# Keeping three more quarter tiles of the KV cache between two layers, two of them in PSUM

## The chip, the cores and the metric

The kernel runs on one core of a Trainium2 chip. A core has a matmul engine (TensorE, PE; its weight loads are listed as PEld), a vector engine (VectorE, DVE), a scalar engine (ScalarE, ACT), a general engine (GpSimd, POOL) and a queue engine that here issues all the DMAs (SyncE, SP). SBUF is the working memory of 128 partitions; PSUM is the memory that matmuls write to, 128 partitions of eight banks of 2 KB. The metric is the device time of one execution in microseconds, lower is better.

## The reference

Two equal layers of a decoder step for a batch of 8, one new token each, width 640, 32 heads of 128, a cache of 4096 positions and one key/value head per query head. Both layers use the same cache and the same weights:

```python
x = x + attention(layernorm(x), k_cache, v_cache, wq, wo)   # q = x @ wq; softmax(q k / sqrt(128)) v; @ wo
x = x + relu(layernorm(x) @ w1) @ w2                         # 640 -> 1728 -> 640
x = x + attention(layernorm(x), k_cache, v_cache, wq, wo)
x = x + relu(layernorm(x) @ w1) @ w2
```

K and V are 268 MB each in bf16. Everything else is small: the weights are 15 MB together. A batch entry's layer 1 needs that entry's layer 0 finished, but different entries do not depend on each other.

## The kernel before

**Tiles.** Heads are taken in 16 pairs (`hp`). K or V of one pair of one batch entry is a tile of 128 partitions x 8192 bf16, 2 MB, cut in four *granules* of 512 KB (4 KB in each partition). On the host the cache is laid out so that the tiles of one entry lie in the order in which they are read. In SBUF lies one `arena` of 26 granule slots; `A_kv` is loaded into it by `do_load(b, p, n, u)`, n granules in a row from place p of entry b into slots u onward. A granule of K costs PE 16 weight loads and 16 matmuls of one column (L490), a granule of V four matmuls of 512 columns in four column groups (L478).

**Visits.** One head pair of one entry in one layer is a visit; there are 256. Layer 0 takes the pairs 0 to 15, layer 1 takes them as 15, 14, 13, 0, 1, ... 12. After layer 0 of entry b come the first four visits of layer 0 of entry b+1, then layer 1 of entry b, then the rest of layer 0 of b+1. The last two entries are cut a little differently, so that layer 0 of the last entry is followed by four visits of the entry before it.

**Around a visit.** The scores of a K tile go to `s_ps` (two buffers). `M1` takes the maxima per partition (DVE), `T` transposes them on PE, `M2` reduces them (DVE), `B` spreads them (PE), `E` makes the exponentials (ACT), `L` and `I` the sums and their reciprocals (PE, DVE). While this chain runs, PE reads the V tile of the visit before. After a V tile `OC` copies the sums out of `o_ps` (ACT), `OG` and `O` gather and scale them, `W` and `Y` apply `wo` and add to x. At the end of an entry's layer 0 the two layernorms and the feed-forward run as *finishing steps*, in pieces of some 15 matmuls between granules, with the inverse root on POOL; then `Q` and `QC` make the queries of layer 1, two visits ahead.

**The order is written by a planner.** `plan()` runs on the host and emits one list of operations. `stream` is the order in which granules are wanted: K of a visit, then V of the visit before. `feed()` walks along it: it takes as many granules as `LEADS` allows for the time by which the modelled load clock is ahead of the modelled PE clock (8 with 9 us of lead, 4 with 6, 2 with 5, else 1), as far as they are neighbours in memory and alike in being kept or not, looks for that many free slots in a row (`room`), and emits one load. If there is no room it stops until the next `release`. `release` is called after each granule's matmuls; it frees the slot unless the granule is kept. All engines execute in the order of this list, so SP's queue is in that order too: a load whose slot is still being read holds up the loads behind it. The DMAs signal through eight semaphores in turn, and a load also waits for the load eight places ahead of it.

**What is kept.** `keep` names granules that stay in their slots from the entry's layer 0 to its layer 1 and are not read a second time. They are `G - SPARE` = 21: V and K of pair 15, V and K of pair 14, V of pair 13 and one granule of K of pair 13. While they lie there, between the end of an entry's layer 0 and the first visits of its layer 1, five slots are left for the first four visits of the next entry.

**PSUM.** Seven of eight banks are used: `o_ps`, two of `s_ps`, and one each of `blk_ps`, `q_ps`, `oy_ps` and `ch_ps`, whose tiles are made anew for each use.

```python
            most = next((n for least, n in LEADS if clock[1] - clock[0] >= least), 1)
            most = min(most, max(1, (len(stream) - at[0]) // 2))
            b, p, keeping = place(stream[at[0]])
```

Of the kernel before, what the change touches and what calls it, by code (L numbers as in the profile page):

```python
# [9 lines left out]
FP32 = mybir.dt.float32  # L10
# [6 lines left out]
UNIT = 4  # L17
GP = 4
G = 26
SPARE = 5  # L20
LEADS = ((9, 8), (6, 4), (5, 2))
AHEAD = 4
CAP = 20


def tile_at(NP, which, hp):

    return max(0, 2 * hp - 1) if which == "K" else min(2 * hp + 2, 2 * NP - 1)


def plan(B, NP, n_up, n_down):
# [18 lines left out]
    assert NV == 2 * B * NP and NP % GP == 0  # L50
    last_of = {(layer, b): v for v, (layer, b, hp) in enumerate(visits)}

    keep = set()
    for hp in order1:
        for which in "VK":
            for g in range(UNIT - 1, -1, -1):
                if len(keep) < G - SPARE:
                    keep.add((which, hp, g))

    slots = []  # L60
    for i in range(NV + 1):
# [22 lines left out]
    def keeps(which, i, g):  # L84
        return visits[i][0] == 0 and (which, visits[i][2], g) in keep

    def place(x):

        return visits[x[1]][1], tile_at(NP, x[0], visits[x[1]][2]) * UNIT + x[2], keeps(*x)

    def room(n):
# [4 lines left out]
    def feed():  # L96

        while at[0] < len(stream):
            most = next((n for least, n in LEADS if clock[1] - clock[0] >= least), 1)
            most = min(most, max(1, (len(stream) - at[0]) // 2))  # L100
            b, p, keeping = place(stream[at[0]])
            n = 1
            while n < most and place(stream[at[0] + n]) == (b, p + n, keeping):
                n += 1
            u = room(n)
            if u is None:
                return
            for k, (which, i, g) in enumerate(stream[at[0] : at[0] + n]):
                ops.extend(("weights",) + w for w in weights.pop(i, []) if which == "K")
                owner[u + k] = True  # L110
                where[which, i, g] = u + k
                if keeping:
                    kept[which, b, visits[i][2], g] = u + k
            clock[1] = max(clock[1], clock[0] + 1.4) + 0.1 + 1.2 * n
            lands[u : u + n] = [clock[1] + 2] * n
            ops.append(("load", b, p, n, u))
            at[0] += n

    def find(which, i, g):
        u = where.get((which, i, g))  # L120
# [2 lines left out]
    def release(which, i, g):  # L123
        key = which, visits[i][1], visits[i][2], g
        u = where.pop((which, i, g), None)
        if key in kept:
            if visits[i][0] == 0:
                return
            u = kept.pop(key)
        at[1] += 1  # L130
        owner[u], freed[u] = False, at[1]
        feed()
# [91 lines left out]
def kernel(  # L224
# [91 lines left out]
    arena = kv.tile([P, G * GW], BF16, name="arena")  # L316
    OR = 96 + CJ
    o_ps = ps.tile([P, CJ * Dh], FP32, name="o_ps")
    nc.vector.memset(o_ps, 0.0)

    up_parts = [range(f, min(f + 3, FC)) for f in range(0, FC, 3)]
# [3 lines left out]
    def ln_steps(b0, nb, xln, key):  # L325
        x = xT[:, b0 : b0 + nb, :]

        def sums():
            s1 = st[key, "s1"] = sm.tile([P, nb], FP32, name="s1", bufs=1)
            nc.vector.tensor_reduce(out=s1, in_=x, axis=AX.X, op=ALU.add)  # L330

        def mean():
            st[key, "mean"] = ps.tile([P, nb], FP32, name="ch_ps")
            nc.tensor.matmul(st[key, "mean"], lhsT=ones_f, rhs=st[key, "s1"], start=True, stop=True)

        def center():
            xc = st[key, "xc"] = sm.tile([P, nb, DC], FP32, name="xc", bufs=1)
            nc.vector.scalar_tensor_tensor(
                out=xc, in0=_free(st[key, "mean"], [(1, nb), (0, DC)]), scalar=-1.0 / D, in1=x, op0=ALU.mult, op1=ALU.add
            )  # L340
            sq = sm.tile([P, nb, DC], FP32, name="sq", bufs=1)
            nc.vector.tensor_tensor(out=sq, in0=xc, in1=xc, op=ALU.mult)
            s2 = st[key, "s2"] = sm.tile([P, nb], FP32, name="s2", bufs=1)
            nc.vector.tensor_reduce(out=s2, in_=sq, axis=AX.X, op=ALU.add)

        def var():
            st[key, "var"] = ps.tile([P, nb], FP32, name="ch_ps")
            nc.tensor.matmul(st[key, "var"], lhsT=ones_f, rhs=st[key, "s2"], start=True, stop=True)  # L348

        def scale():  # L350
            rstd = sm.tile([P, nb], FP32, name="rstd", bufs=1)
            if nb == 1:
                inverse_root(rstd, st[key, "var"])
                nc.gpsimd.tensor_scalar(  # L354
                    out=xln[:, 0, :], in0=st[key, "xc"][:, 0, :], scalar1=rstd, scalar2=None, op0=ALU.mult
                )
            else:
                std = sm.tile([P, nb], FP32, name="std", bufs=1)
                nc.scalar.activation(out=std, in_=st[key, "var"], func=ACT.Sqrt, bias=eps_c, scale=1.0 / D)
# [23 lines left out]
    def finish_steps(layer, b):  # L383
# [5 lines left out]

        def up(k):  # L390
            if k == 0:
                st[key, "h"] = ps.tile([P, FC, nb], FP32, name="ch_ps")
            for f in up_parts[k]:
                fs = f_sizes[f]
                for c in range(DC):
                    nc.tensor.matmul(  # L396
                        st[key, "h"][:fs, f, :], lhsT=w1_sb[:, c, f * P : f * P + fs], rhs=xf[:, :, c],
                        start=(c == 0), stop=(c == DC - 1),
                    )
# [8 lines left out]

        def down(c):
            if c == 0:  # L410
                st[key, "y"] = ps.tile([P, DC, nb], FP32, name="ch_ps")
            for f, fs in enumerate(f_sizes):
                nc.tensor.matmul(
                    st[key, "y"][:, c, :], lhsT=w2_sb[:fs, f, c * P : (c + 1) * P],
                    rhs=st[key, "hT"][:fs, f, :], start=(f == 0), stop=(f == FC - 1),
                )
# [16 lines left out]
    def do_finish(layer, b, k, op):  # L433
# [5 lines left out]
        else:  # L439
            steps[steps[2]][op]()  # L440
            steps[2] = steps[2] or op == "add"

    def do_load(b, p, n, u):
        nc.sync.dma_start(out=arena[:, u * GW : (u + n) * GW], in_=A_kv[b, :, p * GW : (p + n) * GW])

    def do_q0(g):

        q_ps = ps.tile([P, 2 * GP, B], FP32, name="q_ps")
        for h in range(2 * GP):
            for c in range(DC):  # L450
                nc.tensor.matmul(
                    q_ps[:, h, :], lhsT=wq_sb[:, g, c, h * Dh : (h + 1) * Dh], rhs=xln0[:, :, c],
                    start=(c == 0), stop=(c == DC - 1),
                )
        nc.scalar.copy(out=q0[:, g * 2 * GP : (g + 1) * 2 * GP, :], in_=q_ps)

    def do_q(b, hp):
        q_ps = st["q", b, hp] = ps.tile([P, 2], FP32, name="q_ps")
        g, n = divmod(hp, GP)
        for h in range(2):  # L460
            for c in range(DC):
                nc.tensor.matmul(  # L462
                    q_ps[:, h : h + 1], lhsT=wq_sb[:, g, c, (2 * n + h) * Dh : (2 * n + h + 1) * Dh],
                    rhs=xlns[b][:, 0, c : c + 1], start=(c == 0), stop=(c == DC - 1),
                )
# [6 lines left out]
    def do_mm(which, i, g, u):  # L472
# [9 lines left out]
                )  # L482
            return
        if g == 0:
            s_tiles[i] = ps.tile([P, 2 * NJ], FP32, name="s_ps", bufs=2)
        h = 2 * hp + g * 2 // UNIT
        q = q1[b][:, h : h + 1] if layer else q0[:, h, b : b + 1]
        for n in range(GJ):
# [7 lines left out]
        nc.vector.tensor_reduce(out=m_tiles[i], in_=s_tiles[i].rearrange("p (h j) -> p h j", h=2), axis=AX.X, op=ALU.max)  # L496

    def do_t(i):
        blk[i] = ps.tile([P, P + 2 + 2 * NJ], FP32, name="blk_ps")
        nc.tensor.matmul(blk[i][:2, :P], lhsT=m_tiles.pop(i), rhs=ident, start=True, stop=True)  # L500

    def do_m2(i):
# [33 lines left out]
        nc.scalar.copy(out=o_tiles[i][:OR], in_=o_ps[:OR, :].rearrange("p (j d) -> p j d", j=CJ))  # L536

    def do_og(i):
        oy[i] = ps.tile([P, 2 + DC * B], FP32, name="oy_ps")
        for j in range(CJ):  # L540
            nc.tensor.matmul(  # L541
                oy[i][:, :2], lhsT=o_tiles[i][:OR, j, :], rhs=gsel[:OR, j, :], start=(j == 0), stop=(j == CJ - 1)
            )
# [19 lines left out]
    def do_y(i):  # L563
# [2 lines left out]
        y = oy.pop(i)[:, 2 : 2 + DC * nb].rearrange("p (c b) -> p b c", b=nb)  # L566
        nc.vector.tensor_tensor(out=xT[:, b0 : b0 + nb, :], in0=xT[:, b0 : b0 + nb, :], in1=y, op=ALU.add)

    does = dict(load=do_load, weights=load_weights, mm=do_mm, M1=do_m1, T=do_t, M2=do_m2, B=do_b, E=do_e,
                L=do_l, I=do_i, OC=do_oc, OG=do_og, O=do_o, W=do_w, Y=do_y, C=do_finish, Q0=do_q0, Q=do_q, QC=take_q)  # L570

    with tc.manual_schedule(engines={ENG.PE, ENG.DVE, ENG.Activation, ENG.Pool, ENG.SP}):
        xT_ps = ps.tile([P, B * DC], FP32, name="ch_ps")
        nc.tensor.matmul(xT_ps, lhsT=x_bf, rhs=ident[: B * DC, : B * DC], start=True, stop=True)
        nc.vector.tensor_copy(out=xT, in_=xT_ps.rearrange("p (b c) -> p b c", b=B))
        xln0 = consts.tile([P, B, DC], BF16, name="xln0")
# [1 line left out]
            step()  # L578
        for op in ops:
            does[op[0]](*op[1:])  # L580
        r_ps = ps.tile([B * DC, P], FP32, name="ch_ps")
        nc.tensor.matmul(r_ps, lhsT=outT.rearrange("p b c -> p (b c)"), rhs=ident, start=True, stop=True)
        xo = sm.tile([B * DC, P], BF16, name="xo", tag="row", bufs=1)
        nc.vector.tensor_copy(out=xo, in_=r_ps)
# [53 lines left out]
```

## Time and profile before

| | |
|---|---|
| time, median of 3 runs | 2401.72 us (2396.83 to 2401.98) |
| the profiled execution | 2403.26 us, span 2401.5 us |
| TensorE clock granted | 1.0 |
| PE, PEld, DVE, ACT, POOL busy | 1279.5, 786.7, 350.9, 341.2, 43.2 us |
| read from HBM | 1000.66 MB, 417 GB/s over the span |
| loads of the arena | 597, of 1 to 8 granules; 312 of one, 125 of eight |
| issue to landing, median | 6.4 us (one granule), 23.5 (four), 25.0 (eight) |

The page lists busy time by engine, then the span in 40 slices of 60 us with a digit for the busy share in tenths, and for DMA the rate in GB/s. A line of instruction groups reads: line of the program, engine, operation, output and input tiles, count, then busy time and mean, and the idle time before them with what ended it. The chain of work that ended last is followed backwards from the last instruction: at each step to what released it, or to the instruction before it on its engine. A line of the chain in order of time has a start, a duration and what ran; `DMA arena<-in_A_kv_dram` is the time from the issue of a load to its landing. A line of a table of stretches has the stretch, its length, the busy time of each engine with the number of instructions, the granted clock, the busy share of the DMA engines and GB/s.

### The profile page before, as it was taken

How to read it: one execution, taken by the hardware profiler on the slowest of the kernel's cores; microseconds unless marked ns; L12 is line 12 of the kernel's file. 1: busy time of each engine (PE TensorE's matmuls, PEld its weight loads, DVE VectorE, ACT ScalarE, POOL GpSimd, SP SyncE). 2: the span in 40 equal slices, each digit the busy share in tenths (PEclk: the TensorE clock that was granted, in tenths of full speed). 3: DMA queues.
4: the chain of work that ended last, by engine and by line, in shares of the span. 5: the costliest groups of instructions: out<-in, count | busy, mean ns of one | idle time of the engine just before them, and what ended most of it. 6: DMA issues, size and time to landing. Idle time of an engine off the chain costs nothing.

```text
span 2401.5 us, 57352 instructions
## 1 busy us (share of the span) xinstructions
PE 1279.5 (53%) x26486; PEld 786.7 (33%) x26486; DVE 350.9 (15%) x1792; ACT 341.2 (14%) x1179; POOL 43.2 (2%) x198
## 2 busy tenths in 40 slices
PE   3436644475444754447444574445744457445845
PEld 2224322243322532225222352223422234222523
DVE  1101111121111211112111121111111111111211
ACT  1111111111111111111111111111111111111111
POOL 0000000000000000000000000000000000000000
DMA  9999999999999999999999999999999999999997
GB/s 411 431 429 394 429 430 432 428 393 433 430 433 427 371 432 429 432 418 394 434 428 431 416 398 434 430 433 406 413 431 432 430 400 415 431 433 414 406 433 307
DMA packets 87749, 1004.38 MB, mean 418 GB/s; under 512 B 9812, under 2 KB 9812, under 8 KB 49748
## 3 DMA queue, kind: packets, MB, share of 16 engines
q1 hardware_dynamic: 87508, 1000.71, 98.8%
q8 instruction: 207, 3.39, 0.5%
q14 instruction: 34, 0.28, 0.0%
HBM read 1000.66 MB, written 0.01 MB: 417 GB/s over the span
## 4 chain that ended last, share of the span: by engine, by line
DMA 81%; PE 14%; DVE 1%; ACT 1%; issue 1%; POOL 1%; SPq 0%; ACTq 0%; DVEq 0%; POOLq 0%
DMA arena<-in_A_kv_dram 81%; PE o_ps L478 6%; PE s_ps L490 5%; ACT o_sb L536 1%; DVE hmx L504 1%; PE q_ps L462 1%; PE oy_ps L541 1%; PE blk_ps L509 0%; DVE diag L506 0%; PE oy_ps L558 0%; PE blk_ps L500 0%; POOL root L378 0%; DMA wq_sb<-in_A_wq_dram 0%; PE ch_ps L396 0%; PE ch_ps L348 0%
## 5 line engine op out<-in xcount | busy, mean ns | idle before, releaser
L478 PE MATMUL o_ps<-arena,P_sb 128*4 128x512 bf16 x4096 | 562.0, 603 | 506.9 <-DMA arena<-in_A_kv_dram 504.5
L490 PEld LDWEIGHTS <-arena 128*128 128x128 bf16 x16384 | 497.6, 105 | 575.2 <-DMA arena<-in_A_kv_dram 569.0
L490 PE MATMUL s_ps<-q_96,arena 128*128 128x1 bf16 x8192 | 274.0, 165 | 350.1 <-DMA arena<-in_A_kv_dram 346.8
L478 PEld LDWEIGHTS <-P_sb 128*4 128x4 bf16 x4096 | 99.3, 83 | 584.1 <-issue 577.1
L513 ACT ACTIVATE nmax<-blk_ps 128x2 f32<-128x2 f32 x256 | 44.1, 172 | 1702.7 <-PE blk_ps L509 1702.7
L536 ACT CAST o_sb<-o_ps 100x512 bf16<-100x512 f32 x256 | 150.0, 586 | 193.7 <-PE o_ps L478 193.7
L528 DVE TENSOR_REDUCE lsum<-blk_ps 128x2 f32<-128x64 f32 x256 | 57.6, 225 | 731.2 <-PE blk_ps L522 731.2
L496 DVE TENSOR_REDUCE mrow<-s_ps 128x2 bf16<-128x64 f32 x256 | 57.7, 225 | 471.7 <-PE s_ps L490 471.6
L517 ACT ACTIVATE P_sb<-s_ps,nmax 128x32 bf16<-128x32 f32 x512 | 119.3, 284 | 8.2
L504 DVE TENSOR_REDUCE hmx<-blk_ps 2x1 f32<-2x128 f32 x256 | 71.4, 279 | 266.1 <-PE blk_ps L500 265.2
L522 PEld LDWEIGHTS <-onesb_c 128*128 128x128 bf16 x256 | 26.6, 104 | 199.5 <-issue 199.5
L500 PE MATMUL blk_ps<-ident,mrow 128*2 128x128 bf16 x256 | 78.6, 307 | 0.2 <-PE o_ps L478 0.2
L541 PE MATMUL oy_ps<-gsel,o_sb 100*128 100x2 bf16 x1024 | 66.1, 168 | 18.3 <-ACT o_sb L536 0.7
L509 PEld LDWEIGHTS <-onesb_c 2*128 2x128 bf16 x256 | 25.1, 98 | 129.6 <-issue 129.6
L551 DVE TENSOR_TENSOR oT<-oy_ps,invL 128x2 bf16<-128x2 f32 x128 | 20.4, 160 | 321.6 <-PE oy_ps L541 321.6
L522 PE MATMUL blk_ps<-P_sb,onesb_c 128*128 128x64 bf16 x256 | 60.0, 234 | 1.1 <-ACT P_sb L517 1.1
L490 PE MATMUL s_ps<-q_19385,arena 128*128 128x1 bf16 x1024 | 32.8, 166 | 50.7 <-DMA arena<-in_A_kv_dram 50.5
L541 PEld LDWEIGHTS <-o_sb 100*128 100x128 bf16 x1024 | 47.4, 106 | 31.5 <-ACT o_sb L536 31.0
L490 PE MATMUL s_ps<-q_23500,arena 128*128 128x1 bf16 x1024 | 34.0, 166 | 42.1 <-DMA arena<-in_A_kv_dram 41.8
L490 PE MATMUL s_ps<-q_11143,arena 128*128 128x1 bf16 x1024 | 32.6, 166 | 41.5 <-DMA arena<-in_A_kv_dram 41.2
L509 PE MATMUL blk_ps<-diag,onesb_c 2*128 2x2 bf16 x256 | 42.1, 164 | 22.5 <-DVE diag L506 0.2
L462 PE MATMUL q_ps<-xq,wq_sb 128*128 128x1 bf16 x1280 | 52.1, 165 | 3.1 <-POOL xq L354 2.7
(176 smaller groups left out, 703.8 us busy)
## 6 DMA issues: line engine op xcount, KB each, us to landing
arena<-in_A_kv_dram SPq DMA_DIRECT2D x125, 4096.0 KB, 25.0
arena<-in_A_kv_dram SPq DMA_DIRECT2D x104, 2048.0 KB, 23.5
arena<-in_A_kv_dram SPq DMA_DIRECT2D x312, 512.0 KB, 6.4
arena<-in_A_kv_dram SPq DMA_DIRECT2D x41, 1024.0 KB, 11.9
arena<-in_A_kv_dram SPq DMA_DIRECT2D x5, 3584.0 KB, 24.1
arena<-in_A_kv_dram SPq DMA_DIRECT2D x8, 1536.0 KB, 22.4
wq_sb<-in_A_wq_dram SPq DMA_DIRECT2D x4, 1280.0 KB, 29.9
wo_sb<-in_A_wo_dram SPq DMA_DIRECT2D x4, 1280.0 KB, 29.9
```

The costliest lines, as they stand in the source:

```text
L462: nc.tensor.matmul(q_ps[:, h : h + 1], lhsT=wq_sb[:, g, c, (2 * n + h) * Dh : (2 * n + h + 1) * Dh], rhs=xlns[b][:, 0, c : c + 1], start=( ...
L478: nc.tensor.matmul(o_ps[32 * c : 32 * c + CJ, :], lhsT=P_tiles[i][:, h, j : j + CJ], rhs=arena[:, at + c * CJ * Dh : at + (c + 1) * CJ * D ...
L490: nc.tensor.matmul(s_tiles[i][:, j : j + 1], lhsT=arena[:, at + n * P : at + (n + 1) * P], rhs=q, start=True, stop=True)
L496: nc.vector.tensor_reduce(out=m_tiles[i], in_=s_tiles[i].rearrange("p (h j) -> p h j", h=2), axis=AX.X, op=ALU.max)
L500: nc.tensor.matmul(blk[i][:2, :P], lhsT=m_tiles.pop(i), rhs=ident, start=True, stop=True)
L504: nc.vector.tensor_reduce(out=hmx, in_=blk[i][:2, :P], axis=AX.X, op=ALU.max)
L509: nc.tensor.matmul(blk[i][:, P : P + 2], lhsT=ones_b, rhs=nmax.pop(i), start=True, stop=True)
L517: nc.scalar.activation(out=P_tiles[i][:, h, :], in_=S[:, h, :], func=ACT.Exp, bias=nm[:, h : h + 1], scale=inv_sqrt_dh)
L522: nc.tensor.matmul(blk[i][:, P + 2 :], lhsT=ones_p, rhs=P_tiles[i].rearrange("p h j -> p (h j)"), start=True, stop=True)
L528: nc.vector.tensor_reduce(out=L, in_=blk.pop(i)[:, P + 2 :].rearrange("p (h j) -> p h j", h=2), axis=AX.X, op=ALU.add)
L536: nc.scalar.copy(out=o_tiles[i][:OR], in_=o_ps[:OR, :].rearrange("p (j d) -> p j d", j=CJ))
L541: nc.tensor.matmul(oy[i][:, :2], lhsT=o_tiles[i][:OR, j, :], rhs=gsel[:OR, j, :], start=(j == 0), stop=(j == CJ - 1))
```

## The change

- `SPARE` is 4, so 22 granules are kept in the arena, and `STASH` = 2 more granules of each entry are kept in PSUM. The order of what is kept is now K15, K14, V15, K13, V14, V13, from the first granule of each: 22 in SBUF are K15, K14, V15, K13, V14 and two granules of V13; the other two of V13 go to PSUM. No granule of these three pairs is read again for layer 1.
- After the matmuls of a stashed granule in layer 0, `do_stash` copies it to two PSUM tiles (DVE, as int32 with an OR of zero, two instructions of 128x512), and only then is the slot free. When the stream of layer 1 comes to it, `feed` emits `unstash` in place of a load: into a free slot, half by ACT and half by DVE (128x1024 bf16 each).
- The small PSUM tiles are made once and cut from three banks: both halves of `s_ps` in one, `blk_ps` with the queries in the second, `oy_ps` with the layernorm, feed-forward, first and last transposes in the third. With `o_ps` that is four banks; the other four hold the stash.
- The length of a load is also bounded by room: at most a third of the slots that are not kept, less two (8 with nothing kept, 1 with 20 or more).

By the built program there are 625 loads of the arena (333 of one granule, 57 of two, 10 of three, 99 of four, 12 of six, 1 of seven, 113 of eight) against 597, and 1856 granules loaded against 1880. The instructions on PE are the same in number; DVE has 48 more, ACT 16 more (two instructions for each of 16 stashed granules going in, one on each engine coming out).

```diff
@@ -17,9 +17,11 @@
 UNIT = 4
 GP = 4
 G = 26
-SPARE = 5
+SPARE = 4
+STASH = 2
 LEADS = ((9, 8), (6, 4), (5, 2))
 AHEAD = 4
+BANK = 512
 CAP = 20
 
 
@@ -50,12 +52,12 @@
     assert NV == 2 * B * NP and NP % GP == 0
     last_of = {(layer, b): v for v, (layer, b, hp) in enumerate(visits)}
 
-    keep = set()
-    for hp in order1:
-        for which in "VK":
-            for g in range(UNIT - 1, -1, -1):
-                if len(keep) < G - SPARE:
-                    keep.add((which, hp, g))
+    first = [("K", order1[0])]
+    for n in range(3):
+        first += [("K", order1[n + 1])] * (n < 2) + [("V", order1[n])]
+    first = [(which, hp, g) for which, hp in first for g in range(UNIT)]
+    keep = set(first[: G - SPARE])
+    stash = first[G - SPARE : G - SPARE + STASH]
 
     slots = []
     for i in range(NV + 1):
@@ -84,8 +86,15 @@
     def keeps(which, i, g):
         return visits[i][0] == 0 and (which, visits[i][2], g) in keep
 
+    def stashed(which, i, g):
+
+        x = which, visits[i][2], g
+        return stash.index(x) if x in stash else None
+
     def place(x):
 
+        if visits[x[1]][0] and stashed(*x) is not None:
+            return None, stashed(*x), False
         return visits[x[1]][1], tile_at(NP, x[0], visits[x[1]][2]) * UNIT + x[2], keeps(*x)
 
     def room(n):
@@ -97,10 +106,10 @@
 
         while at[0] < len(stream):
             most = next((n for least, n in LEADS if clock[1] - clock[0] >= least), 1)
-            most = min(most, max(1, (len(stream) - at[0]) // 2))
+            most = min(most, max(1, (len(stream) - at[0]) // 2), max(1, (G - len(kept) - 2) // 3))
             b, p, keeping = place(stream[at[0]])
             n = 1
-            while n < most and place(stream[at[0] + n]) == (b, p + n, keeping):
+            while n < most and b is not None and place(stream[at[0] + n]) == (b, p + n, keeping):
                 n += 1
             u = room(n)
             if u is None:
@@ -111,10 +120,14 @@
                 where[which, i, g] = u + k
                 if keeping:
                     kept[which, b, visits[i][2], g] = u + k
+            at[0] += n
+            if b is None:
+                lands[u] = clock[0] + 2
+                ops.append(("unstash", p, u))
+                continue
             clock[1] = max(clock[1], clock[0] + 1.4) + 0.1 + 1.2 * n
             lands[u : u + n] = [clock[1] + 2] * n
             ops.append(("load", b, p, n, u))
-            at[0] += n
 
     def find(which, i, g):
         u = where.get((which, i, g))
@@ -127,6 +140,8 @@
             if visits[i][0] == 0:
                 return
             u = kept.pop(key)
+        if visits[i][0] == 0 and stashed(which, i, g) is not None:
+            ops.append(("stash", stashed(which, i, g), u))
         at[1] += 1
         owner[u], freed[u] = False, at[1]
         feed()
@@ -316,6 +331,11 @@
     arena = kv.tile([P, G * GW], BF16, name="arena")
     OR = 96 + CJ
     o_ps = ps.tile([P, CJ * Dh], FP32, name="o_ps")
+    s_ps = ps.tile([P, 2, 2 * NJ], FP32, name="s_ps")
+    blk_ps = ps.tile([P, BANK], FP32, name="blk_ps")
+    oy_ps = ps.tile([P, BANK], FP32, name="oy_ps")
+    stash_ps = [ps.tile([P, 2 * BANK], BF16, name=f"stash{n}_ps") for n in range(STASH * GW // (2 * BANK))]
+    per = len(stash_ps) // STASH
     nc.vector.memset(o_ps, 0.0)
 
     up_parts = [range(f, min(f + 3, FC)) for f in range(0, FC, 3)]
...
@@ -440,12 +460,25 @@
             steps[steps[2]][op]()
             steps[2] = steps[2] or op == "add"
 
+    def do_stash(slot, u):
+        for n, t in enumerate(stash_ps[slot * per : (slot + 1) * per]):
+            nc.vector.tensor_scalar(
+                out=t.bitcast(mybir.dt.int32),
+                in0=arena[:, u * GW + n * 2 * BANK : u * GW + (n + 1) * 2 * BANK].bitcast(mybir.dt.int32),
+                scalar1=0, scalar2=None, op0=ALU.bitwise_or,
+            )
+
+    def do_unstash(slot, u):
+        for n, t in enumerate(stash_ps[slot * per : (slot + 1) * per]):
+            copy = nc.vector.tensor_copy if n % 2 else nc.scalar.copy
+            copy(out=arena[:, u * GW + n * 2 * BANK : u * GW + (n + 1) * 2 * BANK], in_=t)
+
     def do_load(b, p, n, u):
         nc.sync.dma_start(out=arena[:, u * GW : (u + n) * GW], in_=A_kv[b, :, p * GW : (p + n) * GW])
 
     def do_q0(g):
 
-        q_ps = ps.tile([P, 2 * GP, B], FP32, name="q_ps")
+        q_ps = blk_ps[:, 256 : 256 + 2 * GP * B].rearrange("p (h b) -> p h b", b=B)
         for h in range(2 * GP):
             for c in range(DC):
                 nc.tensor.matmul(
@@ -455,7 +488,7 @@
         nc.scalar.copy(out=q0[:, g * 2 * GP : (g + 1) * 2 * GP, :], in_=q_ps)
 
     def do_q(b, hp):
-        q_ps = st["q", b, hp] = ps.tile([P, 2], FP32, name="q_ps")
+        q_ps = st["q", b, hp] = blk_ps[:, 320:322]
         g, n = divmod(hp, GP)
         for h in range(2):
             for c in range(DC):
@@ -482,7 +515,7 @@
                 )
             return
         if g == 0:
-            s_tiles[i] = ps.tile([P, 2 * NJ], FP32, name="s_ps", bufs=2)
+            s_tiles[i] = s_ps[:, i % 2]
         h = 2 * hp + g * 2 // UNIT
         q = q1[b][:, h : h + 1] if layer else q0[:, h, b : b + 1]
         for n in range(GJ):
@@ -496,7 +529,7 @@
         nc.vector.tensor_reduce(out=m_tiles[i], in_=s_tiles[i].rearrange("p (h j) -> p h j", h=2), axis=AX.X, op=ALU.max)
 
     def do_t(i):
-        blk[i] = ps.tile([P, P + 2 + 2 * NJ], FP32, name="blk_ps")
+        blk[i] = blk_ps[:, : P + 2 + 2 * NJ]
         nc.tensor.matmul(blk[i][:2, :P], lhsT=m_tiles.pop(i), rhs=ident, start=True, stop=True)
 
     def do_m2(i):
@@ -536,7 +569,7 @@
         nc.scalar.copy(out=o_tiles[i][:OR], in_=o_ps[:OR, :].rearrange("p (j d) -> p j d", j=CJ))
 
     def do_og(i):
-        oy[i] = ps.tile([P, 2 + DC * B], FP32, name="oy_ps")
+        oy[i] = oy_ps[:, : 2 + DC * B]
         for j in range(CJ):
             nc.tensor.matmul(
                 oy[i][:, :2], lhsT=o_tiles[i][:OR, j, :], rhs=gsel[:OR, j, :], start=(j == 0), stop=(j == CJ - 1)
...
```

More of the change, by code (lines that the diff above doesn't have):

```diff
@@ L332, in mean @@
         def mean():
-            st[key, "mean"] = ps.tile([P, nb], FP32, name="ch_ps")
+            st[key, "mean"] = oy_ps[:, 64 : 64 + nb]
             nc.tensor.matmul(st[key, "mean"], lhsT=ones_f, rhs=st[key, "s1"], start=True, stop=True)
@@ L346, in var @@
         def var():
-            st[key, "var"] = ps.tile([P, nb], FP32, name="ch_ps")
+            st[key, "var"] = oy_ps[:, 72 : 72 + nb]
             nc.tensor.matmul(st[key, "var"], lhsT=ones_f, rhs=st[key, "s2"], start=True, stop=True)
@@ L391, in up @@
             if k == 0:
-                st[key, "h"] = ps.tile([P, FC, nb], FP32, name="ch_ps")
+                st[key, "h"] = oy_ps[:, 128 : 128 + FC * nb].rearrange("p (f b) -> p f b", b=nb)
             for f in up_parts[k]:
@@ L410, in down @@
             if c == 0:
-                st[key, "y"] = ps.tile([P, DC, nb], FP32, name="ch_ps")
+                st[key, "y"] = oy_ps[:, 256 : 256 + DC * nb].rearrange("p (c b) -> p c b", b=nb)
             for f, fs in enumerate(f_sizes):
@@ L567, in do_y @@
         nc.vector.tensor_tensor(out=xT[:, b0 : b0 + nb, :], in0=xT[:, b0 : b0 + nb, :], in1=y, op=ALU.add)
-    does = dict(load=do_load, weights=load_weights, mm=do_mm, M1=do_m1, T=do_t, M2=do_m2, B=do_b, E=do_e,
+    does = dict(load=do_load, stash=do_stash, unstash=do_unstash, weights=load_weights, mm=do_mm, M1=do_m1, T=do_t, M2=do_m2, B=do_b, E=do_e,
                 L=do_l, I=do_i, OC=do_oc, OG=do_og, O=do_o, W=do_w, Y=do_y, C=do_finish, Q0=do_q0, Q=do_q, QC=take_q)
     with tc.manual_schedule(engines={ENG.PE, ENG.DVE, ENG.Activation, ENG.Pool, ENG.SP}):
-        xT_ps = ps.tile([P, B * DC], FP32, name="ch_ps")
+        xT_ps = oy_ps[:, : B * DC]
         nc.tensor.matmul(xT_ps, lhsT=x_bf, rhs=ident[: B * DC, : B * DC], start=True, stop=True)
@@ L580 @@
             does[op[0]](*op[1:])
-        r_ps = ps.tile([B * DC, P], FP32, name="ch_ps")
+        r_ps = oy_ps[: B * DC, :P]
         nc.tensor.matmul(r_ps, lhsT=outT.rearrange("p b c -> p (b c)"), rhs=ident, start=True, stop=True)
```

## The prediction

> **What bounds the kernel now.** I read the page first: DMA is in the top tenth in every slice but the last, TensorE is busy for 53%, and the chain that ended last is 81% the arrival of `arena` loads.
>
> ```profile
> span 2401.5 us, 57352 instructions
> PE 1279.5 (53%) x26486; PEld 786.7 (33%) x26486; DVE 350.9 (15%) x1792; ACT 341.2 (14%) x1179; POOL 43.2 (2%) x198
> ...
> DMA  9999999999999999999999999999999999999997
> GB/s 411 431 429 394 429 430 432 428 393 433 430 433 427 371 432 429 432 418 394 434 428 431 416 398 434 430 433 406 413 431 432 430 400 415 431 433 414 406 433 307
> ...
> DMA 81%; PE 14%; DVE 1%; ACT 1%; issue 1%; POOL 1%; SPq 0%; ACTq 0%; DVEq 0%; POOLq 0%
> ...
> arena<-in_A_kv_dram SPq DMA_DIRECT2D x312, 512.0 KB, 6.4
> ```
>
> So bytes decide, with a ripple: about every 300 us the rate falls from 430 to some 390 GB/s. Next I asked for stretches: 45 us and 30 us at the ripples, and a long one between two (columns after the times: busy us of PE, PEld, DVE, ACT, POOL with counts, clock, DMA share, GB/s).
>
> ```profile
> 492.00:537.00 45.00, 34.42 (x701) 23.30 (x698) 9.06 (x48) 7.00 (x26) 5.30 (x24) 1.00 1.00 387
> 785.00:830.00 45.00, 32.60 (x653) 22.07 (x650) 8.43 (x45) 6.84 (x25) 5.31 (x24) 1.00 0.98 369
> 245.00:490.00 245.00, 121.15 (x2492) 71.60 (x2491) 33.40 (x168) 34.98 (x120) 0.00 (x0) 1.00 1.01 431
> ```
> ```profile
> 500.00:530.00 30.00, 22.54 (x451) 15.96 (x452) 5.60 (x31) 4.23 (x16) 5.30 (x24) 1.00 1.03 407
> 1088.00:1118.00 30.00, 21.09 (x395) 14.43 (x395) 5.38 (x29) 4.07 (x15) 5.30 (x24) 1.00 0.98 382
> ```
>
> There are eight such stretches, one per batch entry: the time in which that entry's kept granules lie in the arena while layer 0 of the next entry streams through what is left. All eight 45 us stretches (380, 387, 369, 382, 378, 394, 390, 396) average 384.5 GB/s, a loss of 45 x (1 - 384.5/431) = 4.9 us each, 39 us in all. Outside them the rate is 431 GB/s whatever PE does, and a granule of 524,288 bytes costs 1.216 us. The core of the tight stretch is all single-granule loads through five slots: eight 30 us stretches (396, 407, 384, 382, 392, 403, 389, 398) average 393.9 GB/s, 1.331 us a granule.
>
> What limits it there is in the chain, from 505 to 523 us (start, duration, what):
>
> ```profile
> 503.34 5.83 DMA arena<-in_A_kv_dram
> 509.17 0.05 issue
> 509.22 0.60 PE s_ps L490 x16
> 509.82 0.02 issue
> 509.84 6.50 DMA arena<-in_A_kv_dram
> 516.34 0.04 issue
> 516.38 0.60 PE o_ps L478 x4
> 516.98 0.04 PE blk_ps L522
> 517.02 5.45 DMA arena<-in_A_kv_dram
> ```
>
> That is one slot going round: a load takes 5.5 to 6.5 us from issue to landing, PE reads it in 0.60, and 0.67 us after the landing the next load into that slot is issued. The page's median for all 312 single loads, 6.4, says the same. Five slots at 1.331 are a round of 6.66 us: 0.67 and a mean latency of 5.99.
>
> **The change part by part.**
>
> *Fewer bytes.* Kept per entry: 21 granules before, 22 in SBUF and 2 in PSUM after. The built program's loads sum to 1880 and 1856 granules: 24 x 1.216 = **-29.2 us**. Excess reads of layer 1 disappear where the queue was full (the 431 GB/s rows), so the saving is whole.
>
> *One slot fewer in the tight stretch.* With 22 kept, four slots remain. By the built order 24 loads per entry run strictly in this mode (from the load released by the second K tile of the next entry to the last before layer 1 frees slots); each waits until PE has read the granule four places ahead, so a round must fit in 4 x 1.216 = 4.87 us to cost nothing, i.e. latency up to 4.20. The upper end is that latency stays 5.99: 6.66/4 = 1.665 us a granule. The lower end: the shortest single load of this trace took 4.2 us (the one issued at 1673.5; another at 205.15 took 4.3), so 4.9/4 = 1.23, and then no worse than the 1.331 of now; fewer slots cannot make the same stage faster. I take the middle mechanism: with four slots a load queues behind three others instead of four, so latency drops by one transfer, 5.99 - 1.22 = 4.77, nearer to the 4.58 that the chain has for the load issued at 498.08 than to 5.99. Round 5.44, 1.36 a granule. To this 0.03 for late releases by PE: in the tight stretches some 5% of releases come 1.2 us or more after the landing instead of 0.67 (finishing steps stand between), and a four-slot round has little to absorb that. 1.39 - 1.331 = 0.06; 24 x 0.06 x 8 = **+11 us**; ends 0 and 24 x 0.334 x 8 = +64.
>
> On that round the Trainium skill speaks with two voices (DMA: Bandwidth & Descriptors). Its section "Anatomy of one DMA" fits 2.0 us + bytes/436 GB/s per DMA on the GpSimd path, an estimate of 3.2 us for a granule: a round of 3.9, no cost, and a sum 11 us lower. Its section "Bandwidth" asks for DMAs of at least 1 MiB to reach 75% of peak, which speaks against a mode of 512 KB loads: at 327 GB/s a granule would be 1.60 us, the mode +52 us, and the change slower. The rows have such loads at 382 to 407 GB/s with five in flight, so neither is taken.
>
> *Loads shortened by room.* Ahead of a tight stretch the loads now come as 6, 4, 3, 2 and 1 granules instead of 8 and 4; singles go from 312 to 333. Wire time is unmoved within the rows (431 in stretches of 8s; up to 437 in slices of single loads). At the entry it could gain: the 45 us stretches lose 4.9, their 30 us cores 30 x (1 - 393.9/431) = 2.6, so up to 2.3 us per entry (18 us in all) lie at its edges, where PE must work off a four-granule arrival before it frees slots. I take 0 and keep -18 as the low end.
>
> *Stash and unstash.* Per entry four DVE copies of 128x512 int32 into PSUM, and two ACT and two DVE copies of 128x1024 back. No such copy is in the trace. Each DVE copy: from 0.48 (the 128x512 memset at L319) to about 0.60 (0.225 for 64 columns at L528, 0.279 for 128 at L504, extended). Each copy back: about 1.0, from the 0.586 for 512 at L536 and 0.17 for 2 at L513. So some 2.4 us of DVE going in, 2 + 2 coming out, 51 us over the run, on engines at 15% and 14%. Coming in, the slot's next load is issued 1.2 us later and everything behind it on SP's queue too; cover: twelve granules (14.6 us) are issued ahead of it there. Coming out, M2 of one visit waits about 1 us behind the DVE copy, E behind ACT's, then PE's L and the next K tile; cover: the six to ten singles issued as the layer-1 tile from SBUF frees slots, 7 us. Uncovered it would be 8 x 2 = 16 us. I take 0.
>
> *Tiles sharing PSUM banks.* The built order has waits that cross tiles of a bank: 105 query matmuls wait for DVE, 112 T matmuls for ACT, 254 M1 reductions for ACT, and 231 waits of T on PE itself go. Each is at most one short operation, 0.16 (L470) to 0.28 (L504): 105 x 0.28 + 112 x 0.16 = 47 us of PE if nothing covered it, and down to the same size gained from the waits that go. But PE waits for DMA for 548 us at the scores and 504 at the values, and in the tight stretch only layer 0 runs, where T's new wait and most Q steps don't occur. 0.
>
> *Start, weights, tail.* The last load of the stream lands about 16 us before the end in both; the order of work behind it is the same. 0.
>
> *Sum.* The profiled execution took 2403.26 (span 2401.5), 1.5 above the median. 2403.3 - 29.2 + 11.3 = 2385.4; against the median **2384**, 0.7% faster. About 0.2% (4.8 us) is what a measurement of this kernel can tell from no change.
>
> **The rivals.**
>
> *Latency does not shrink (slower).* If the 6 us is the memory's and not the queue's, the round stays 6.66 and the mode costs +64: 2401.7 - 29.2 + 64 = 2437. It turns against the change from 29.2/192 + 1.331 = 1.483 us a granule, a round of 5.93, a latency of 5.26. For it: single loads hardly ever landed below 4.6, median 6.4; instruction fetches delay one DMA engine at a time and a shallow queue hides that less. Against: five in flight come at 1.22 to 1.25 us for long runs, which is the engines' own pace, so most of the 6 us is queueing.
>
> *PE becomes the bound in the tight stretch (slower or same).* PE is busy 22.5 of 30 us there, and ten finishing steps of about 0.55 us (15 matmuls of 0.167 at L396 and L413 with their loads) stand between granules. If four slots leave each of them exposed: 8 x 10 x 0.55 = +44, 2417. Half of them exposed with the 11 above: 2404, no change. Against: releases nearly always came 0.67 after the landing, so PE was waiting.
>
> *No cost and a smoother entry (much faster).* 2401.7 - 29.2 - up to 18: 2354 to 2372. For it: the edge losses above; against: every slot less can only hurt in the core.
>
> **How the numbers follow.** Forecast case (2372 to 2396) 0.55; much faster 0.15; no change 0.10; slower, by either mechanism, 0.20. So faster 0.70, same 0.10, slower 0.20. The range 2366 to 2412 leaves out about 0.06 below and 0.10 above; the likeliest case alone is 2372 to 2396.
>
> **What would show it.** HBM read of 988.1 MB and 24 granules less; steady stretches still 431 GB/s; tight stretches with four slots at 370 to 385 GB/s (1.36 to 1.42 us a granule) and single loads landing in 4.6 to 5.0 us. A median of 5.5 or more, or under 350 GB/s there, makes the slower rival right. Copies at 0.5 to 0.6 and 1.0 us, with no wait of PE for them over 2 us. If the chain's `arena` share falls while PE's grows in the tight stretch, it was PE.

## The result and the profile after

The changed kernel takes 2411.46 us, median of 4 runs (2408.21 to 2417.75), against 2401.19 (2396.83 to 2401.98) for the kernel before: a ratio of 1.005, 95% interval 1.0026 to 1.0074. It is slower by half a per cent; the forecast was 0.7% faster.

The page of the changed kernel, the lines that answer to those of before:

```profile
span 2410.6 us, 57884 instructions
PE 1284.3 (53%) x26486; PEld 781.0 (32%) x26486; DVE 379.0 (16%) x1840; ACT 354.5 (15%) x1195; POOL 42.8 (2%) x198
...
GB/s 412 430 430 364 425 429 430 428 360 432 428 433 426 356 433 430 431 424 358 434 429 433 404 366 431 432 431 398 385 433 430 431 384 397 431 430 409 372 432 307
...
HBM read 988.08 MB, written 0.01 MB: 410 GB/s over the span
...
arena<-in_A_kv_dram SPq DMA_DIRECT2D x333, 512.0 KB, 6.1
```

The bytes are gone as forecast, 12.6 MB. The plateau of the rate is unmoved, 430 GB/s. The dips are deeper: the lowest slice of each was 371 to 406 GB/s and is now 356 to 385. The same stretches as before, moved by the few us that the kernel has shifted, and one chain in such a stretch:

```profile
502.00:532.00 30.00, 19.51 (x370) 13.58 (x369) 4.70 (x26) 3.31 (x13) 4.40 (x21) 1.00 0.98 344
1098.00:1128.00 30.00, 20.68 (x422) 14.34 (x420) 5.89 (x27) 5.54 (x19) 2.63 (x12) 1.00 0.95 334
260.00:480.00 220.00, 105.79 (x2196) 61.68 (x2192) 31.03 (x151) 30.36 (x104) 0.00 (x0) 1.00 1.01 431
```
```profile
503.74 5.93 DMA arena<-in_A_kv_dram
509.67 0.05 issue
509.72 0.58 PE s_ps L523 x16
510.33 5.60 DMA arena<-in_A_kv_dram
515.97 0.60 PE o_ps L511 x4
516.61 5.04 DMA arena<-in_A_kv_dram
521.65 0.05 issue
521.70 0.59 PE s_ps L523 x16
522.32 5.76 DMA arena<-in_A_kv_dram
```

PE is no later than before: each round still has 0.6 us of it, and PE is busy for 20.0 of the 30 us where it was 22.1 (means of the eight stretches). The load itself takes 5.0 to 5.9 us, with one load fewer in front of it. The column to read is GB/s and not the busy share of the DMA engines: that share has moved only from 1.01 to 0.96 (means of the eight), since a packet of 4 KB takes 185 ns there in the mean where it took 166. The eight 30 us stretches of this kernel (340, 344, 340, 334, 327, 344, 342, 339) average 338.8 GB/s, 1.548 us a granule, against 1.331 before. 24 granules x 8 x 0.217 = +41.7 us; with the -29.2 of the bytes that is +12.5, where the spans differ by 2410.6 - 2401.5 = +9.1. The rest, -3, lies just ahead of the stretches. Load by load in the two traces, the time beyond 1.216 us a granule, summed over the single-load cores and the 30 granules ahead of each, is 31.8 us before and 68.3 after: +36.5.

### The profile page after: what moved, and what is told of

The parts are those of the page before. It is cut to its first block, busy times and chain, and to the rows that moved or that the text cites. A ratio compares the mean times of both kernels' runs of the same rounds, so it can differ in the third digit from the quotient of the medians.

```text
span 2410.6 us, 57884 instructions
## 1 busy us (share of the span) xinstructions
PE 1284.3 (53%) x26486; PEld 781.0 (32%) x26486; DVE 379.0 (16%) x1840; ACT 354.5 (15%) x1195; POOL 42.8 (2%) x198
## 4 chain that ended last, share of the span: by engine, by line
DMA 83%; PE 13%; ACT 1%; DVE 1%; issue 1%; POOL 0%; SPq 0%; ACTq 0%; DVEq 0%
DMA arena<-in_A_kv_dram 82%; PE o_ps L511 5%; PE s_ps L523 5%; ACT o_sb L569 1%; DVE hmx L537 1%; PE blk_ps L495 1%; PE oy_ps L574 1%; DVE diag L539 0%; PE oy_ps L591 0%; PE blk_ps L533 0%; PE blk_ps L542 0%; ACT arena L474 0%; DMA wq_sb<-in_A_wq_dram 0%; PE blk_ps L555 0%; PE oy_ps L433 0%
## 5 line engine op out<-in xcount | busy, mean ns | idle before, releaser
L523 PE MATMUL s_ps<-q_96,arena 128*128 128x1 bf16 x8192 | 274.1, 166 | 416.4 <-DMA arena<-in_A_kv_dram 410.6
L511 PEld LDWEIGHTS <-P_sb 128*4 128x4 bf16 x4096 | 93.2, 81 | 567.9 <-issue 561.2
L533 PE MATMUL blk_ps<-ident,mrow 128*2 128x128 bf16 x256 | 70.7, 276 | 0.0
L495 PE MATMUL blk_ps<-xq,wq_sb 128*128 128x1 bf16 x1280 | 52.0, 165 | 2.9 <-POOL xq L374 1.3
L591 PE MATMUL oy_ps<-oT,wo_sb 128*128 128x1 bf16 x1280 | 52.0, 165 | 0.2 <-issue 0.2
L523 PE MATMUL s_ps<-q_2856,arena 128*128 128x1 bf16 x1024 | 32.6, 165 | 34.8 <-DMA arena<-in_A_kv_dram 33.8
L591 PEld LDWEIGHTS <-wo_sb 128*128 128x128 bf16 x1440 | 49.7, 104 | 1.0 <-issue 1.0
```

What stands on the lines that cost most here:

```text
L495: nc.tensor.matmul(q_ps[:, h : h + 1], lhsT=wq_sb[:, g, c, (2 * n + h) * Dh : (2 * n + h + 1) * Dh], rhs=xlns[b][:, 0, c : c + 1], start=( ...
L511: nc.tensor.matmul(o_ps[32 * c : 32 * c + CJ, :], lhsT=P_tiles[i][:, h, j : j + CJ], rhs=arena[:, at + c * CJ * Dh : at + (c + 1) * CJ * D ...
L523: nc.tensor.matmul(s_tiles[i][:, j : j + 1], lhsT=arena[:, at + n * P : at + (n + 1) * P], rhs=q, start=True, stop=True)
L591: nc.tensor.matmul(oy[i][:, 2 + c * nb : 2 + (c + 1) * nb], lhsT=wo_sb[:, 2 * hp + h, c * P : (c + 1) * P], rhs=o1[:, 2 * hp + h, :] if la ...
```

## The experiments

The theory after this comparison: the loss is the round of a slot (latency, PE, next issue) shared by four slots in place of five, and nothing else in the change. The rivals: the copies into and out of PSUM, PE or DVE held up by the shared PSUM banks, and the shortened loads.

**Five slots.** Only the number is changed; the stash, the packed banks and the shortened loads stay.

```diff
-SPARE = 4
+SPARE = 5
```

> The changed kernel with SPARE 5: five slots are left in the tight stretch, 21 granules are kept in SBUF and 2 in PSUM, 1864 granules are loaded. Theory (the whole loss is the round of four slots, 1.55 us a granule against 1.33): the tight core is back at 1.33, 390 to 400 GB/s, and the 16 granules less than before (16 x 1.216 = 19.5 us) come out whole: 2401 - 19.5 = 2382. Rival (stash copies, shared PSUM banks or the shortened loads cost the time): the 38 us of loss stay, 2401 - 19.5 + 38 = 2420.

Measured: 2377.25 us, ratio 0.9913 (0.9892 to 0.9934). The kernel before took 2397.41 us beside it (2397.4 to 2401.4 in the five groups of runs of this study, which is why ratios are compared across groups). Faster than both kernels. One slot given back is 33 us against the changed kernel by the two ratios, although eight granules more are loaded. Two of its stretches:

```profile
492.00:522.00 30.00, 22.40 (x438) 15.89 (x436) 5.37 (x30) 3.31 (x13) 4.53 (x21) 1.00 1.00 393
783.00:813.00 30.00, 21.69 (x425) 15.54 (x421) 5.46 (x30) 3.31 (x13) 4.31 (x20) 1.00 0.99 374
```

The second is below the 390 to 400 that were expected, but the single loads of all eight cores come every 1.31 us, where those of the kernel before come every 1.36. Stash, banks and short loads are all still in it, so none of them holds the loss.

**Six slots.** `SPARE = 6` in the same place.

> The changed kernel with SPARE 6: six slots in the tight stretch, 20 granules kept in SBUF and 2 in PSUM, 1872 loaded (8 x 1.216 = 9.7 us less than before). Theory of the round: latency and turn of five slots, 5.9 + 0.8, over six give 1.12, under the wire time of 1.22, so the core runs at 1.25 to 1.28 and gains 24 x 0.06 x 8 = 12 us more: 2379, about level with five slots. If a further slot brings nothing (stalls of single DMA engines set the 1.33): 2391. Rival of stash or banks: 2430.

Measured: 2373.02 us, ratio 0.9896 (0.9875 to 0.9917), the fastest kernel of this study. The next slot is still worth more than the granule that it displaces. Two stretches of it, and two turns of its chain:

```profile
490.00:520.00 30.00, 22.17 (x435) 16.02 (x435) 5.70 (x31) 3.90 (x14) 2.65 (x12) 1.00 1.01 395
780.00:810.00 30.00, 22.75 (x439) 16.12 (x438) 5.86 (x32) 3.48 (x13) 2.94 (x14) 1.00 1.01 397
```
```profile
503.28 8.10 DMA arena<-in_A_kv_dram
511.38 0.04 issue
511.42 0.62 PE o_ps L511 x4
512.05 0.02 issue
512.07 6.67 DMA arena<-in_A_kv_dram
```

Here the load takes 6.7 to 8.1 us and the stretch is faster all the same: with six in flight the rate itself is the limit (the table below has 1.28 us a granule, and hardly less with a seventh) and the latency is a queue. That is the state which I had assumed for five.

**Only the packed banks.** What is kept, the loads and their order are those of before, no stash.

```diff
-SPARE = 4
-STASH = 2
+SPARE = 5
+STASH = 0
...
-    keep = set(first[: G - SPARE])
-    stash = first[G - SPARE : G - SPARE + STASH]
+    keep = set()
+    for hp in order1:
+        for which in "VK":
+            for g in range(UNIT - 1, -1, -1):
+                if len(keep) < G - SPARE:
+                    keep.add((which, hp, g))
+    stash = []
...
-            most = min(most, max(1, (len(stream) - at[0]) // 2), max(1, (G - len(kept) - 2) // 3))
+            most = min(most, max(1, (len(stream) - at[0]) // 2))
...
-    per = len(stash_ps) // STASH
+    per = 0
```

> Only the packing of the small PSUM tiles: what is kept, the loads and their order are those of before, with no stash. Theory: the waits across a bank are covered, no change, 2401, and the tight core stays at 1.33 us a granule. Rival (shared banks make PE late): up to 2401 + 38 = 2439.

Measured: 2400.19 us, ratio 1.001 (0.9998 to 1.0022). The waits that now cross the tiles of a bank (471 by the prediction's count for the changed kernel) cost nothing that stands clear of zero, and at most 5 us by the interval.

**Only four slots.** The kernel before, with `SPARE = 5` made 4 and nothing else.

> The kernel before with SPARE 4 and nothing else: 22 granules kept, four slots, own PSUM tiles, no stash, loads not bounded by room; 1872 loaded. Theory of the round: 2401 - 9.7 + 24 x 0.217 x 8 = 2433, core at 1.55 us a granule. Rival (stash, banks or load sizes): 2401 - 9.7 = 2392, core at 1.33.

Measured: 2433.24 us, ratio 1.0145 (1.0126 to 1.0164). That it meets 2433 to the microsecond is luck: the kernel before ran at 2397.41 beside it, so the loss is 36 us where the theory had 32. Its tight stretches are those of the changed kernel:

```profile
503.00:533.00 30.00, 18.84 (x367) 13.70 (x367) 4.90 (x27) 2.67 (x10) 2.98 (x14) 1.00 0.97 334
800.00:830.00 30.00, 18.54 (x363) 13.45 (x363) 4.50 (x25) 2.68 (x10) 2.65 (x12) 1.00 0.95 318
```

Load by load, counted as above, the cores and the 30 granules ahead of them lose 70 us here and 68 in the changed kernel; with five slots they lose 32 (the kernel before) and 24 (the changed kernel with five). So four slots alone make the loss, with and without the rest of the change. What was left is why the latency fell by so much less than a transfer.

**Three slots and two.** `SPARE` of 3 and 2 in the changed kernel; the stash shrinks to one granule and to none, the bytes stay.

> The changed kernel with SPARE 3: three slots in the tight stretch, 23 granules kept in SBUF and 1 in PSUM, the bytes of the changed kernel (1856 granules). Asked is what the 5.5 us of latency with four slots are. Theory of a floor (about 5 us are there with little queued): latency 5.0 to 5.2, round 5.8, 1.93 us a granule, 2411 + 192 x 0.38 = 2485. Rival of the prediction (queueing, one transfer of 1.2 us less for each slot taken away): latency 4.3, 1.66 us a granule, 2411 + 192 x 0.11 = 2433.

> The changed kernel with SPARE 2: two slots in the tight stretch, 24 granules kept in SBUF, none in PSUM, the same 1856 granules. Floor: latency about 5.0, 2.84 us a granule, 2411 + 192 x 1.29 = 2660. Queueing: latency at the 4.2 of the shortest load, 2.44 us a granule, 2411 + 192 x 0.89 = 2582.

One execution each: 2480.1 and 2604.88 us. Three slots came close to the time of the floor, though the latency (4.83 us in the table below) was under its 5.0 to 5.2; two came nearer to the rival. Neither was right. The chain with two slots (each load has at most one other in front of it):

```profile
538.17 4.13 DMA arena<-in_A_kv_dram
542.30 0.05 issue
542.35 0.58 PE s_ps L523 x16
542.93 0.03 PE oy_ps L591 x2
542.97 4.07 DMA arena<-in_A_kv_dram
547.03 0.05 issue
547.08 0.60 PE s_ps L523 x16
```

The table goes through the single loads of the eight cores, from issue and landing in each trace. Counted is a load whose slot was filled before it by a single load as many places ahead as there are slots: 24 per core (22 or 24 in the kernel before, 21 with seven slots). The means are:

| slots | latency, us | landing to next issue, us | from issue to issue, us a granule |
|---|---|---|---|
| 2 | 4.26 | 0.67 | 2.43 |
| 3 | 4.83 | 0.68 | 1.81 |
| 4 (the changed kernel) | 5.46 | 0.68 | 1.51 |
| 5 (the kernel before) | 6.03 | 0.70 | 1.36 |
| 5 (the changed kernel with five) | 5.84 | 0.71 | 1.31 |
| 6 | 6.96 | 0.71 | 1.28 |
| 7 | 8.19 | 0.71 | 1.27 |

(The 30 us stretches, cut at fixed times, gave 1.548 for four slots and 1.331 for five.) Up to five slots the latency rises by 0.4 to 0.6 us a slot, not by the 1.2 of a transfer, and latency and next issue together, divided by the slots, give the pace within 2%. From five to seven it rises by 0.9 to 1.2 a slot and the pace hardly moves: only there does a load wait for nearly whole transfers of others.

**Fewer instruction fetches.** The instructions themselves come over the DMA engines (207 packets of 16 KB in the changed kernel, 0.94 us each), each on one of the 16 engines. Could they make the 5.5 us?

```diff
-        for n in range(GJ):
-            j = g * GJ + n
-            nc.tensor.matmul(
-                s_tiles[i][:, j : j + 1], lhsT=arena[:, at + n * P : at + (n + 1) * P], rhs=q, start=True, stop=True
-            )
+        j = g * GJ
+        nc.tensor.matmul(
+            s_tiles[i][:, j : j + GJ], lhsT=arena[:, at : at + P], rhs=_free(q, [(0, GJ)]), start=True, stop=True
+        )
```

> The changed kernel (four slots) with one score matmul of 16 columns for each K granule in place of 16 matmuls of one; fifteen of sixteen blocks of keys are left out of the computation, the loads stay. PE has 15/16 fewer instructions in K, so fewer instruction fetches on the DMA engines, and a K granule's slot is freed some 0.45 us earlier. If the fetches make the latency: 5.5 falls to 5.1 or less, 1.39 us a granule, about 2381. If they do not: latency stays 5.4 to 5.5, the earlier release alone gives (5.5 + 0.47)/4 = 1.49 us a granule and about 2400.

One execution: 2379.95 us. The line of the fetches (packets, MB, share of the engines' time) in the changed kernel and here:

```profile
q8 instruction: 207, 3.39, 0.5%
q8 instruction: 87, 1.43, 0.2%
```

In the tight core the latency is 5.45 us as before, landing to next issue 0.48, 1.46 us a granule. But there the fetches fell only from 32 to 18, so the run alone does not acquit them, and the loads of the changed kernel say more when they are split. The 113 of 192 with a fetch in flight beside them took 5.73 us, the 79 without one 5.07. A load has landed when the last of its sixteen shares has, and that one came 0.63 us after the fifteenth with a fetch, 0.26 without (144 loads have all sixteen landings in the trace). With five slots (the changed kernel with five) the same split is 5.92 and 5.64. So the fetches are a part of the latency with four slots, about 0.4 us of 5.46, and not the whole: (5.07 + 0.68)/4 is still 1.44 us a granule.

The time as a whole fell by 31 us, and both kernels issue the same 625 loads in the same order, so the traces show where. Of 32 us between the spans 11 lie in the tight cores and 21 outside them, where I had expected no change, nearly all of it among the long loads. Past the first twenty loads, of the 209 of four granules or more that follow another of at least two, 28 land more than 0.3 us late in the changed kernel, 25 us in all, and 10 here, 6 us. Of the 28, 27 had a fetch in their time; of the 88 loads without a fetch one was late. That speaks for the fetches as the cost outside the core, though the run shortened PE's work together with them. The agreement of the time with the first expectation is no evidence for its reason, since most of the gain is elsewhere.

**Seven slots.** `SPARE = 7`, which loads exactly the bytes of the kernel before.

> The changed kernel with SPARE 7: seven slots, 19 granules kept in SBUF and 2 in PSUM, 1880 granules loaded, the bytes of the kernel before. Theory of the round: with seven slots the wire alone sets the core, 1.23 to 1.24 us a granule against 1.27 with six; the six-slot kernel's 2373 + 9.7 for bytes - 6 = 2377. It shows the optimum: under 2373 would mean that stalls were still open at six.

Measured: 2383.9 us, ratio 0.9931 (0.9909 to 0.9953). The core is at 1.27, where six have 1.28. By the medians seven slots are 10.9 us slower than six, by the ratios 8.4, and the eight granules cost 9.7: the slot was worth nothing that can be told. Six is the best of the numbers tried.

**Long loads with six slots.** The bound on a load's length by room is taken out of the six-slot kernel.

```diff
-            most = min(most, max(1, (len(stream) - at[0]) // 2), max(1, (G - len(kept) - 2) // 3))
+            most = min(most, max(1, (len(stream) - at[0]) // 2))
```

> The six-slot kernel without the bound on a load's length by room (loads of 8 and 4 up to the tight stretch, as before). It tells what the shortened loads are worth at the edges of the tight stretch, for which I had taken 0 and a gain of 2.3 us per entry at most. If they smooth the entry: 2373 + 8 x 1 to 2.3 = 2381 to 2391. If they are worth nothing: 2373.

Measured: 2373.09 us against 2373.02 with the bound. The shortened loads are worth nothing at six slots.

**A shorter tight stretch.** `AHEAD = 3` in the six-slot kernel.

> The six-slot kernel with three visits of the next entry between an entry's layers in place of four: the tight stretch is eight granules shorter. By the round alone: 8 x 8 x (1.27 - 1.22) = 3 us less, 2370. Rival: the finishing steps have one visit less to fit in, PE waits for the queries of layer 1 at the end of each, and the time rises by the wait, up to some 2 us per entry, 2386.

Measured: 2424.77 us, ratio 1.0109 (1.0092 to 1.0126). The rival was right and its price far too small. Between the last granule of the stretch and the first of layer 1 the chain now runs through the end of the feed-forward, two layernorm reductions, the inverse root and the queries, with no load in it:

```profile
519.04 1.56 PE oy_ps L433 x42
520.63 0.17 DVE xT L440
...
526.13 0.20 POOL rstd L400
526.43 0.32 POOL xq L374
526.79 0.42 PE blk_ps L495 x10
527.24 0.17 ACT q L503
527.45 0.56 PE s_ps L523 x16
```

That is 8.4 us from the 42 matmuls to the first scores, and the same at the two other entries read (816.03 to 824.43, 1408.82 to 1417.23); the time rose by 52 us, 6.5 per entry. The fourth visit is what hides it.

**Six slots without PSUM.** The kernel before with `SPARE = 6`.

> The kernel before with SPARE 6 and nothing else: six slots, 20 granules kept, no stash, 1888 loaded. It separates what the better kernel owes to the sixth slot from what it owes to PSUM. From five to six slots with the stash the time went from 2377 to 2373 with 9.7 us more of bytes, so the slot was worth 14: 2401 + 9.7 - 14 = 2397. If the stash were what helps the core: 2401 + 9.7 = 2411.

Measured: 2395.69 us, ratio 0.9984 (0.9974 to 0.9993). The sixth slot almost pays for its bytes without any stash. The six-slot kernel with the stash is 21 (by the ratios) to 23 us faster; its 16 granules less are 19.5 of these.

## Why the prediction was wrong

The sum failed in one term, "One slot fewer in the tight stretch": +11 us were taken, and the stretches show +41.7, the count load by load +36.5. The step that fell is "with four slots a load queues behind three others instead of four, so latency drops by one transfer, 5.99 - 1.22 = 4.77". The latency fell by 0.4 to 0.6 us, from 6.03 (5.84 in the changed kernel with five slots) to 5.46. A whole transfer comes off only where the wire is full (1.2 us from seven slots to six, 0.4 to 0.6 a slot from five down), and with five slots it was not. My own row had the core at 393.9 GB/s beside a plateau of 431, so some 9% of the rate was missing there, though the busy share of the DMA engines was 1.01. The words "five in flight come at 1.22 to 1.25 us for long runs" described the good runs between the stalls, not the mean. Read as it stood, the round of 6.66 was already the limit at five, and taking a slot away had to cost much of its share: in proportion 25%, measured 16% (1.331 to 1.548). The row that I took for support, 4.58 us at 498.08, is a load issued after a pause of 5.5 us, and DMA moved 209 GB/s in the us after it; the shortest loads of the trace are not the latency of a steady stretch. What keeps the latency up is settled in part: instruction fetches are some 0.4 us of it by the split above. Why the latency without a fetch, too, falls by less than a transfer (5.64 with five slots, 5.07 with four) stays open.

The mechanism was named on the losing side. "Latency does not shrink" had the condition right (it turns at a latency of 5.26; measured 5.46) and its price of 2437 too high because the latency did shrink a little. Its sign, under 350 GB/s in the tight stretch, came (338.8). Its reason that instruction fetches delay one engine and a shallow queue hides that less is borne out in part: a fetch goes with 0.66 us more at four slots and 0.28 at five. With 0.20 for all slower cases I gave it too little.

The other terms held. Bytes: -29.2 us expected, 12.6 MB read less at an unmoved plateau. Shared banks: 0, and the packing alone measures 1.001. Shortened loads: 0, and without them nothing moves at six slots. Late releases by PE: I had added 0.03 us a granule for them; the landing-to-issue time is 0.68 with four slots and 0.70 with five, so there was nothing to add. PE as the bound: refuted by the same number and by PE's smaller share; half of that cost with the 11 us makes 2406, not the 2404 that I wrote. The last load lands 14.5 us before the end in both, not 16, and the term is 0 all the same. The copies:

```profile
L465 DVE TENSOR_SCALAR stash_ps<-arena x32: 682/685/695, 182.9 to 2207.7; 128x512 int32<-128x512 int32 x32
L474 ACT COPY arena<-stash_ps x16: 1012/1015/1018, 243.3 to 2265.2; 128x1024 bf16<-128x1024 bf16 x16
L474 DVE COPY arena<-stash_ps x16: 691/692/693, 243.3 to 2265.3; 128x1024 bf16<-128x1024 bf16 x16
```

The copies in took 0.685, above my bounds of 0.48 and 0.60; those out 1.015 on ACT, as estimated, and 0.69 on DVE against 1.0. With five slots the kernel that has them gains 20.2 us where its bytes alone promise 19.5, so they cost nothing that the time shows.

On the Trainium skill (DMA: Bandwidth & Descriptors): the estimate of 3.2 us for a granule from its section "Anatomy of one DMA", a fit for the GpSimd path, lies below the 4.1 us that the chain shows here, and the mean of 4.26, for loads issued by SP with at most one other in flight (the shortest of them took 3.4). Its section "Bandwidth" with the 1 MiB rule would, by an estimate (75% of 436), have put the mode at 327 GB/s or less; four in flight gave 339, six gave 395 with the same size. What decided was how many loads were in flight, not how long one was.

## What to carry to other kernels

Before a buffer is taken from a stream, compare the rate of the stretch where it is scarcest with the plateau: if it is already below, suspect the round trip as the limit; here the latency then shrank by half of a transfer at most, and the stretch slowed by two thirds of what proportion to the buffers would give. Price a buffer as a slot in flight against what it saves as storage: here a granule kept saved 9.7 us in all, the fifth slot was worth 43 to 45, the sixth 14, the seventh nothing that can be told (time gained by the ratios and the granules' bytes added back). When both are changed at once, run the count of slots alone as a sweep; the best point here (six slots, two granules in PSUM) is 1.0% below the kernel before, on the other side of it from the change.

## What the runs showed of the hardware

A 512 KB load into 128 partitions, issued from SP, took 4.26 us from issue to landing in the mean with two in flight, and 0.4 to 0.6 us more for each further one up to five, while the rate was below the plateau; it took six in flight (3 MB) to come to 1.28 us a granule, where long loads need 1.22. The busy share of the DMA engines does not show this: it was 1.01 at 394 GB/s and 0.96 at 339. A load lands with the last of its sixteen shares: in the cores of the changed kernel the first came 3.5 us after the issue and the last 5.1 where no instruction fetch was in flight. Where one was, the last came at 5.7. Leaving out fifteen of sixteen score matmuls, which took the instruction fetches from 207 to 87 and nothing from the loads, made the run 31 us shorter, some 19 of them among the long loads; there 27 of 121 loads with a fetch in their time landed more than 0.3 us late, and 1 of 88 without. That goes with the fetches, but a run that changes them alone was not made.
